# Two edits to a one-core attention and two-MLP kernel: other buffers for the last evacuations of the first MLP, and four of sixteen weight-conversion units issued in its last block

## The chip, the core and the metric

The kernel runs on one core of a Trainium2 chip. Five engines work side by side, each in its own program order: PE (TensorE matmuls; its weight loads are listed as PEld), DVE (VectorE), ACT (ScalarE), POOL (GpSimd) and SP (SyncE, which here only issues transfers). They wait for each other through semaphores. The metric is the device time of one execution in microseconds (us). Lower is better.

## The reference, cut to what matters

```python
# attention: 4 batches, 8 heads, 576 tokens, head size 64; block-causal mask in blocks of 64
scores = scale * np.matmul(q, k.transpose(0, 1, 3, 2))
scores = np.where(block_i >= block_j, scores, -1000000000.0)
attn = np.exp(scores - max); attn = attn / (sum(attn) + 1e-09)
x = np.matmul(attn, v)             # as a 2304 x 512 matrix
# first MLP: 512 -> 2048 -> 512
r = np.maximum(x @ w_in, 0.0)
x = (s * (r * r) + b) @ w_out
# second MLP: 512 -> 2048 -> 512, other weights
h = x @ w2_in
out = np.maximum(0.01 * h, h) @ w2_out
```

All arrays are float32. The kernel splits each matmul operand into a high part and a rest and adds three products, so that the result has float32 accuracy.

## The kernel before, in words

**Blocks.** The 2304 tokens are cut into five blocks by token position: four of 512 tokens (128 positions of each of four batches) and one of 256. `ORDER = (0, 1, 2, 4, 3)` gives the order in which they are worked on; here they are called by their place in that order, so block 3 is the one of 256 tokens and block 4, the last, again has 512. In each block the first MLP walks over 16 chunks `f` of the 2048 inner features. `m_in` (L864) computes `h` (twelve matmuls: four pieces of `x`, three products each), ACT and DVE turn it into `g = relu(h)^2`, `gh` (the high part) and `gl` (the rest), and `m_out` (L903) adds `gh` and `gl` times the output weights into four PSUM banks `y0` to `y3`. While block `k` runs its MLP, the attention of block `k + 1` is woven between its matmuls (`later_block`). The last block has no attention beside it.

**End of a block.** After the 16th chunk the four `y` banks are scaled and copied to SBUF tiles `yo` (`evac`, L477, on ACT or DVE, whichever the planner picks), and each `yo` tile is stored to the DRAM tensor `yT` (L936). The `yo` tiles come from the pool `st`, which has two buffers.

**Second weights.** The second MLP uses a Winograd form of Strassen's scheme (seven products in place of eight), so its weights are needed in combined blocks. Sixteen "units" (`units`, L392) prepare them while the first MLP runs. A unit takes a slot of the pool `stg` (two buffers of 16 KB per partition), loads 64-bit words with four transfers (L417), decodes them (DVE L424, L427, L433; ACT L430), makes four combined blocks (DVE L441), splits them (ACT L447, DVE L448) and stores them to `u_in` (L453) or `u_out` (L458). Units 0 to 3 and 8 to 11 make input weights (`u_in`), units 4 to 7 and 12 to 15 output weights (`u_out`) of the first and the second half of the features.

**Second MLP.** It runs six steps (three groups of 768 tokens, two feature halves each). Its tiles `G`, `gh2`, `gl2`, `Y` and `w2` are in pools that are opened after the pools of the first MLP are closed (`G.gate`, near the end), in the same SBUF space on the left side: from low to high addresses `stg`, `gh`, `gl`, `g`, `st`, `xh`, `xl` before, and `w2`, `gh2`, `gl2`, `Y`, `G` after. A tile that takes over the bytes of an older one waits until the older one's last reader is done, and a store is a reader until it has landed. `load_units` (L965) loads the combined weights (`wi`, `wo`), and `x_load` loads `yT` back as `xr`.

**Order.** No engine's order is written by hand. Every operation is a `Step` with a due time; `Graph.order` (L87) walks an event list with assumed durations and, for each engine that is free, issues the ready step with the earliest due time. For steps that open a buffer of a pool, a free buffer must be there. The instructions then stand in that order on their engines, and a wait at the head of an engine's queue holds up all behind it.

Of the kernel before, what the change touches and what calls it, by code (L numbers as in the profile page):

```python
# [8 lines left out]
F32 = mybir.dt.float32  # L9
# [182 lines left out]
NB = 5  # L192
# [4 lines left out]
def kernel(  # L197
# [19 lines left out]
    NF = w1_out.shape[0] // 128  # L217
# [6 lines left out]
    KEEP = 4  # L224
    NH = 384
    WS = 12
    BACK = 20.0

    def sb(name, bufs):
        return ctx.enter_context(tc.tile_pool(name=name, bufs=bufs))  # L230
# [33 lines left out]
    def buf(key, shape, dt=F32, tag=None):  # L264
        return Buf(key, lambda: pools[key][0].tile(shape, dt, tag=key, name=tag or key))

    def bank(key, name):
        return buf(key, [128, 512], F32, name)
# [16 lines left out]
    begin, ut, t = [], [], 30.0  # L285
# [6 lines left out]
    def at(k, f):  # L292
        return begin[k] + f * ut[k]
# [5 lines left out]
    w_t, w_ok = {}, {}  # L299
# [67 lines left out]
    def walk(blk):  # L367
        return range(NF) if blk % 2 == 0 else range(NF - 1, -1, -1)

    def weights_at(blk, pos, f):  # L370

        if not blk:
            return
        if pos < NF - KEEP:
            w_t[blk, f] = w_t[blk - 1, f]
            for i in range(2):
                w_ok[blk, f, i] = w_ok[blk - 1, f, i]
            return
        slot = f if f < KEEP else f - NF + 2 * KEEP
        w = w_t[blk, f] = buf("w", [128, 4, 512], F32R, "w")  # L380
        a = G.add(
            {"SP": 0.65}, lambda e: e.dma_start(out=w().bitcast(F32).rearrange("p a n -> p (a n)"), in_=kept[slot]),
            [kept_ok[f], done[blk, pos - NF + KEEP]], [w], [], at(blk, pos) - 30, nbytes=1048576)
        for i in range(2):
            w_ok[blk, f, i] = a
# [3 lines left out]
    OUT7 = ("S1", "S2", "S3", "S4", "A11", "A12", "A22")  # L389
    unit_ok = {}  # L390

    def units():  # L392

        seq = [(half, kind, i) for half in range(2) for kind in range(2) for i in range(4)]
        t0, t1 = begin[1] - 15, begin[NB] - 40
        stored = w_ok[0, NF - 1, 1]
        for n, (half, kind, i) in enumerate(seq):
            due = t0 + (n + 1) * (t1 - t0) / len(seq)
            slot = buf("stg", [128, 2, 2, 1024], F32, "unit")
            f1 = 8 * half + 2 * i  # L400
            at8 = (IN7, OUT7)[kind]
# [2 lines left out]
            blk = lambda x, slot=slot, names=names: slot()[:, 1, :, 128 * names.index(x):128 * names.index(x) + 128]  # L404
# [44 lines left out]
            st = []  # L449
# [27 lines left out]
    def evac(e, out, in_, by=1.0):  # L477
        if e is nc.scalar:
            e.activation(out=out, in_=in_, func=ACTF.Copy, scale=by)  # L479
        elif isinstance(by, float):  # L480
            e.tensor_copy(out=out, in_=in_)
        else:
            e.tensor_scalar(out=out, in0=in_, scalar1=by, scalar2=None, op0=ALU.mult)

    def both(n):
        return {"ACT": act(n), "DVE": dve(n)}
# [94 lines left out]
    for i in range(WARM + FILL):  # L581

        n = 128 if i < WARM else 256
# [46 lines left out]
    for p in range(NP):  # L630
        due = 10.0 + 4.0 * p
# [14 lines left out]
        o = bank("s", "o")  # L646
# [200 lines left out]
    def x_split(blk, c):  # L847

        k = ORDER[blk]
        T = TB[k]  # L850
        xf, ok = xf_t[k, c], xf_ok[k, c]
        x_open(blk, c)
        h, l = xh_t[blk, c], xl_t[blk, c]
        due = begin[blk] - 1
        hi = G.add({"ACT": act(T)}, lambda e: e.activation(out=h()[:, :T], in_=xf()[:, :T], func=ACTF.Copy), ok, [h], [xf], due)
        lo = G.add(
            {"DVE": dve(T)}, lambda e: e.tensor_tensor(out=l()[:, :T], in0=xf()[:, :T], in1=h()[:, :T].bitcast(F32), op=ALU.subtract),  # L857
            [hi], [l], [h, xf], due, port=True,
        )
        x_ok[blk, c] = [hi, lo]  # L860
# [40 lines left out]
    done = {}  # L901

    def m_out(blk, f, pos):  # L903
        k = ORDER[blk]
        T = TB[k]
        w = w_t[blk, f]
        W = T + 2 * (k == NB - 1)
        gh, gl, hi, lo = g_t[blk, f]
        due = at(blk, pos) + 1.5 * unit[k]
        for d in range(KD):  # L910
            if pos == 0:
                y_t[blk, d] = bank(f"y{d}", "y")
            y = y_t[blk, d]

            def fn(e, d=d, y=y):
                for n, (wi, x) in enumerate(((2, gh), (3, gh), (2, gl))):
                    e.matmul(  # L917
                        out=y()[:, :W], lhsT=w()[:, wi, d * 128:(d + 1) * 128], rhs=x()[:, :W],
                        start=(pos == 0 and n == 0), stop=(pos == NF - 1 and n == 2),
                    )  # L920

            a = G.add(
                {"PE": 3 * (T / 2400 + 0.013)}, fn, [hi, lo, w_ok[blk, f, 1], y_last.get((blk, d))],
                [y] * (pos == 0), [y, w, gh, gl], due + d * 0.01,
            )
            y_last[blk, d] = a
            if pos < NF - 1:
                continue
            o = buf("st", [128, 512], F32, "yo")
            ev = G.add(both(T), lambda e, o=o, y=y: evac(e, o()[:, :T], y()[:, :T], s_sb), [a, *sb_ok], [o], [y], due)  # L930
            if k == NB - 1:
                c_ok.append(G.add({"DVE": 0.2}, lambda e, y=y, d=d: e.tensor_scalar(
                    out=c_sb[:, d:d + 1], in0=y()[:, T:T + 1], scalar1=b_sb, scalar2=None, op0=ALU.mult), [a, *sb_ok], uses=[y], due=due))
            rows = slice(d * 128, (d + 1) * 128)
            y_st[k, d] = G.add(
                {"SP": 0.65}, lambda e, o=o, rows=rows: e.dma_start(out=yT[rows, T0[k]:T0[k] + T], in_=o()[:, :T]),  # L936
                [ev], uses=[o], due=due, nbytes=512 * T,
            )
        done[blk, pos] = a

    units()
    for blk in range(NB):
        if blk:
            for c in range(KD):
                x_split(blk, c)
        for pos, f in enumerate(walk(blk)):
            weights_at(blk, pos, f)
            m_in(blk, f, pos)
            m_out(blk, f, pos)
# [298 lines left out]
```

## Time and profile before

| | |
|---|---|
| median of 3 runs | 981.56 us (979.61 to 983.95) |
| profiled execution, its own time | 977.85 us |
| its span, first to last instruction | 975.9 us |
| PE busy | 942.3 us (97%) |
| PE weight loads busy | 828.6 us (85%) |
| DVE busy | 657.4 us (67%) |
| ACT busy | 576.3 us (59%) |
| mean granted TensorE clock | 0.995 of full speed |

Busy times are of one profiled execution on the hardware. A line number is that of the kernel before; `x3` after a row is the number of instructions merged into it, and in square brackets stands how long the engine had been idle and what ended that.

### The profile page before, as it was taken

Reading aid. Unit: us, or ns where it says so; the run is one execution under the profiler, and the core shown is the slowest. Engines: PE = TensorE matmul, PEld = TensorE weight load, DVE = VectorE, ACT = ScalarE, POOL = GpSimd, SP = SyncE. Lnnn points to the kernel's source line nnn. Section 1 sums busy time; section 2 is a strip of 40 time slices with the busy share of each in tenths; the row PEclk is TensorE's granted clock in tenths of the full one; section 3 lists DMA queues with packets and bytes.
Section 4 is the critical chain, followed back from the end, with each engine's and each line's share of the span. In section 5 each row is a group of like instructions: output and inputs, shape, how many; then the busy total and the mean of one; then the engine's idle time right before and its main releaser. Section 6 shows DMA issues by size and latency. Waiting matters only on the chain. (4 is left out here: it accounts for less than half of the span.)

```text
span 975.9 us, 16708 instructions
## 1 busy us (share of the span) xinstructions
PE 942.3 (97%) x5780; PEld 828.6 (85%) x5780; DVE 657.4 (67%) x1343; ACT 576.3 (59%) x1247; POOL 106.2 (11%) x231
## 2 busy tenths in 40 slices
PE   9899999999999999998999998899989999899998
PEld 8688887777778888786778887899979999799998
DVE  5888868668878687886866422456595565955657
ACT  4787757566677566876765321554564545645443
POOL 1122211111112131132220000000000000000000
PEclk9999999999999999999999999899999999999999
DMA  8994386976688967799745446774115751157402
GB/s 227 342 347 133 127 258 201 361 221 211 196 262 267 321 212 244 233 294 266 196 120 195 178 159 233 293 284 178 57 34 183 282 179 57 33 185 282 171 1 66
DMA packets 143828, 197.26 MB, mean 202 GB/s; under 512 B 23296, under 2 KB 118144, under 8 KB 137088
## 3 DMA queue, kind: packets, MB, share of 16 engines
q1 hardware_dynamic: 141296, 195.41, 61.1%
q10 hardware_dynamic: 2448, 0.79, 0.4%
q8 instruction: 46, 0.75, 0.3%
q14 instruction: 38, 0.31, 0.1%
HBM read 148.96 MB, written 47.19 MB: 201 GB/s over the span
## 5 line engine op out<-in xcount | busy, mean ns | idle before, releaser
L874 PE MATMUL h<-xh,w 128*128 128x512 f32 (+1 forms) x640 | 231.1, 390 | 5.1 <-DVE g L888 3.5
L917 PE MATMUL y<-gh,w 128*128 128x512 f32 (+1 forms) x640 | 186.0, 374 | 0.2 <-ACT gh L892 0.2
L874 PEld LDWEIGHTS h<-xh,w 128*128 128x128 f32 x640 | 118.4, 189 | 31.3 <-issue 5.2
L917 PEld LDWEIGHTS y<-gh,w 128*128 128x128 f32 x640 | 114.5, 188 | 22.2 <-issue 2.3
L1147 ACT ACTIVATE gh<-G 128x384 fp32r<-128x384 f32 x168 | 86.8, 524 | 59.1 <-PE A L1154 25.5
L1001 DVE TENSOR_TENSOR gl<-G,gh 128x384 fp32r<-128x384 f32 x168 | 92.5, 554 | 43.3 <-PE A L1154 18.7
L1088 PE MATMUL A<-xh,wi 128*128 128x384 f32 x384 | 112.9, 337 | 6.6 <-ACT G L1063 6.6
L874 PE MATMUL h<-xl,w 128*128 128x512 f32 (+1 forms) x320 | 118.5, 370 | 0.6 <-DVE xl L857 0.6
L917 PE MATMUL y<-gl,w 128*128 128x512 f32 (+1 forms) x320 | 118.5, 370 | 0.3 <-DVE l L763 0.3
L1154 PE MATMUL A<-gh,wo 128*128 128x384 f32 x384 | 98.4, 337 | 1.5 <-ACT gh L1147 1.5
L890 ACT ACTIVATE g<-h 128x512 f32<-128x512 f32 (+1 forms) x80 | 44.4, 554 | 85.5 <-PE h L874 78.9
L1088 PEld LDWEIGHTS A<-xh,wi 128*128 128x128 f32 x384 | 71.1, 189 | 7.0 <-ACT G L1063 6.9
L563 PE MATMUL t<-id_sb,p 128*128 128x128 f32 x400 | 66.6, 280 | 5.2 <-POOL p L765 1.9
L1154 PEld LDWEIGHTS A<-gh,wo 128*128 128x128 f32 x384 | 69.0, 188 | 2.8 <-ACT gh L1147 2.1
L917 PEld LDWEIGHTS y<-gl,w 128*128 128x128 f32 x320 | 60.2, 188 | 11.1 <-issue 0.4
L1103 ACT ACTIVATE G<-G 128x384 f32<-128x384 f32 x72 | 37.8, 525 | 52.1 <-DVE G L1068 52.1
L563 PEld LDWEIGHTS t<-id_sb,p 128*128 128x128 f32 x400 | 47.9, 142 | 22.0 <-issue 4.8
L874 PEld LDWEIGHTS h<-xl,w 128*128 128x128 f32 x320 | 60.6, 189 | 6.9 <-DVE xl L857 0.8
L1154 PE MATMUL A<-gl,wo 128*128 128x384 f32 x192 | 64.7, 337 | 0.4
L479 ACT ACTIVATE pt<-t 128x512 f32<-128x512 f32 (+2 forms) x80 | 42.4, 533 | 37.9 <-PE t L563 37.1
L1088 PE MATMUL A<-xl,wi 128*128 128x384 f32 x192 | 64.7, 337 | 0.0
L888 DVE TENSOR_TENSOR g<-g,h 128x512 f32<-128x512 f32 (+1 forms) x38 | 25.3, 665 | 54.8 <-ACT g L890 54.6
(125 smaller groups left out, 1894.3 us busy)
## 6 DMA issues: line engine op xcount, KB each, us to landing
wi<-u_in SPq DMA_DIRECT2D x32, 896.0 KB, 4.6
wo<-u_out SPq DMA_DIRECT2D x28, 1024.0 KB, 6.1
w<-kept SPq DMA_DIRECT2D x16, 1024.0 KB, 7.3
u_in<-unit SPq DMA_DIRECT2D x16, 896.0 KB, 5.7
u_out<-unit SPq DMA_DIRECT2D x32, 448.0 KB, 4.6
early<-in_moe_w_in_dram SPq DMA_DIRECT2D x16, 512.0 KB, 5.8
early<-in_moe_w_out_dram SPq DMA_DIRECT2D x16, 512.0 KB, 6.4
kept<-w SPq DMA_DIRECT2D x8, 1024.0 KB, 6.5
```

What stands on the lines that cost most here:

```text
L479: e.activation(out=out, in_=in_, func=ACTF.Copy, scale=by)
L563: e.transpose(tb()[:, x * 128:(x + 1) * 128], P()[:, pc:pc + 128], id_sb)
L874: e.matmul(out=h()[:, :T], lhsT=w()[:, wi, c * 128:(c + 1) * 128], rhs=x[blk, c]()[:, :T], start=(c == 0 and n == 0), stop=(c == KD - 1 an ...
L888: e.tensor_tensor(out=g()[:, :T], in0=g()[:, :T], in1=h()[:, :T], op=ALU.mult)
L890: a = G.add({"ACT": act(T)}, lambda e: e.activation(out=g()[:, :T], in_=h()[:, :T], func=ACTF.Relu), [prev], [g], [h], due)
L917: e.matmul(out=y()[:, :W], lhsT=w()[:, wi, d * 128:(d + 1) * 128], rhs=x()[:, :W], start=(pos == 0 and n == 0), stop=(pos == NF - 1 and n ...
L1001: e.tensor_tensor(out=out, in0=x, in1=y, op=ALU.subtract)
L1088: e.matmul(out=x()[:, :NH], lhsT=in_w[n, i, c]()[:, s, ai], rhs=y(), start=(first and c == 0 and m == 0), stop=(c == 1 and m == 2), skip_g ...
L1103: {"ACT": act(NH)}, lambda e, y=y: e.activation(out=y(), in_=y(), func=ACTF.Lrelu), [a], [], [y], d2 + 2)
L1147: hi = G.add({"ACT": act(NH)}, lambda e, gh=gh, x=x: e.activation(out=gh(), in_=x(), func=ACTF.Copy), [a], [gh], [x], due - 2)
L1154: e.matmul(out=z[d]()[:, :NH], lhsT=out_w[n, r]()[:, 2 * i + d, s], rhs=y(), start=(first and i == 0 and m == 0), stop=(i == 3 and m == 2) ...
```

## The change

There are two edits.

The four `yo` tiles of the last block come from the pool `xl` (four buffers) and no longer from `st` (two buffers). `xl` holds the rests of the block's input `x`, which `m_in` of the last chunk reads for the last time.

`units` is cut in two calls. Units 0 to 11 are added before the blocks, with due times spread between a little before block 1 and a little before block 3. Units 12 to 15 are added at block 4, with due times spread over block 4; their loads wait in addition for the step `done[NB - 2, 12]`, the last `m_out` matmul of the 13th chunk of block 3. The constant `BACK`, which nothing uses, goes.

```diff
-    BACK = 20.0
+    UNITS = 12
...
-    def units():
+    def units(which, stored):
 
         seq = [(half, kind, i) for half in range(2) for kind in range(2) for i in range(4)]
-        t0, t1 = begin[1] - 15, begin[NB] - 40
-        stored = w_ok[0, NF - 1, 1]
-        for n, (half, kind, i) in enumerate(seq):
-            due = t0 + (n + 1) * (t1 - t0) / len(seq)
+        first = (0, UNITS, len(seq))
+        spans = ((begin[1] - 15, begin[3] - 10), (begin[4] + 4, begin[5] - 6))
+        for n, (half, kind, i) in enumerate(seq[first[which]:first[which + 1]]):
+            due = spans[which][0] + (n + 1) * (spans[which][1] - spans[which][0]) / (first[which + 1] - first[which])
             slot = buf("stg", [128, 2, 2, 1024], F32, "unit")
...
-            o = buf("st", [128, 512], F32, "yo")
+            o = buf("st" if blk < NB - 1 else "xl", [128, 512], F32, "yo")
...
-    units()
+    units(0, w_ok[0, NF - 1, 1])
     for blk in range(NB):
+        if blk == NB - 1:
+            units(1, done[NB - 2, 12])
         if blk:
```

Since the planner sets the order, the change moves instructions on every engine from block 1 on. Three places follow. From the end of the first MLP on, PE's order is the same in both, row for row; the lines after the edit have moved by two numbers (L1063 is L1065, and so on).

ACT at the end of the last block, before (`g`, `gh`: last chunk; `yo`: evacuations; `G`: first tiles of the second MLP):

```order
L890 ACTIVATE g<-h 128x512
L892 ACTIVATE gh<-g 128x512
L479 ACTIVATE yo<-y,s_sb 128x512
L1063 ACTIVATE G<-A 128x384
L1063 ACTIVATE G<-C 128x384
L1103 ACT_TABLE_LOAD
L1103 ACTIVATE G<-G 128x384
```

and with the change:

```order
L890 ACTIVATE g<-h 128x512
L892 ACTIVATE gh<-g 128x512
L479 ACTIVATE yo<-y,s_sb 128x512 x2
L1065 ACTIVATE G<-A 128x384
L1065 ACTIVATE G<-C 128x384
L1105 ACT_TABLE_LOAD
L1105 ACTIVATE G<-G 128x384
```

ACT now does two of the four evacuations and DVE two, where it was one and three. Listed with its waits, the first `G<-A` waits for four transfers before, and for none with the change; in the program before, that `G` tile lies over both buffers of `st`. With the change the fifth to the tenth `G` tile lie over buffers of `xl`, and there a transfer is waited for.

SP at the end of block 3, before (`v`, `k`, `q`: attention loads; `unit`: loads of a unit; `u_out`: its stores; `yT`: stores of the block's result; `xr`: loads of the second MLP's first input):

```order
L708 DMA k<-in_k_dram 64x512 x2
L716 DMA v<-in_v_dram 128x4x128 x2
L458 DMA u_out<-unit 128x7x128 x4
L716 DMA v<-in_v_dram 128x4x128
L936 DMA yT<-yo 128x256 x2
L1023 DMA xr<-yT 128x384 x4
L936 DMA yT<-yo 128x256 x2
```

and with the change:

```order
L708 DMA k<-in_k_dram 64x512 x4
L716 DMA v<-in_v_dram 128x4x128 x2
L417 DMA unit<-in_moe_w_out_dram 128x2x256 x8
L716 DMA v<-in_v_dram 128x4x128
L936 DMA yT<-yo 128x256 x3
L1025 DMA xr<-yT 128x384
L936 DMA yT<-yo 128x256
```

The stores of the last unit are gone from here, and the eight loads of units 12 and 13 stand between the second-last and the last `v` load.

DVE from the end of block 3 into block 4, before (`xf`, `xl`: input of block 4; `c_sb`: a bias; `l`, `p`: softmax):

```order
L765 TENSOR_SCALAR p<-p,l 128x512
L857 TENSOR_TENSOR xl<-xf,xh 128x512 x3
L893 TENSOR_TENSOR gl<-g,gh 128x256
L481 COPY xf<-o 128x256
L483 TENSOR_SCALAR yo<-y,s_sb 128x256
L932 TENSOR_SCALAR c_sb<-y,b_sb 128x1
L483 TENSOR_SCALAR yo<-y,s_sb 128x256
L932 TENSOR_SCALAR c_sb<-y,b_sb 128x1 x3
L857 TENSOR_TENSOR xl<-xf,xh 128x512
L483 TENSOR_SCALAR yo<-y,s_sb 128x256 x2
L888 TENSOR_TENSOR g<-g,h 128x512
L893 TENSOR_TENSOR gl<-g,gh 128x512
```

and with the change:

```order
L427 SCALAR_TENSOR_TENSOR unit<-unit 128x1024
L441 TENSOR_TENSOR unit<-unit 128x2x128
L483 TENSOR_SCALAR yo<-y,s_sb 128x256
L857 TENSOR_TENSOR xl<-xf,xh 128x512
L448 TENSOR_TENSOR unit<-unit 128x2x896
L888 TENSOR_TENSOR g<-g,h 128x512
L433 SCALAR_TENSOR_TENSOR unit<-unit 128x2x512
L893 TENSOR_TENSOR gl<-g,gh 128x512
L441 TENSOR_TENSOR unit<-unit 128x2x128 x4
L893 TENSOR_TENSOR gl<-g,gh 128x512
L448 TENSOR_TENSOR unit<-unit 128x2x896
L893 TENSOR_TENSOR gl<-g,gh 128x512
```

Operations of units 12 and 13 now stand between the steps that feed the first chunks of block 4. Units 14 and 15 follow in the same way later in the block.

## Rows read from the trace of the kernel before

**Rows 1.** Busy time by stretch: length, engines' busy us (instructions), PE clock, DMA share, GB/s

```profile
405.00:515.00 110.00, 101.08 (x895) 85.00 (x895) 81.69 (x193) 74.11 (x174) 29.44 (x63) 0.98 0.75 218
515.00:605.00 90.00, 90.00 (x407) 75.22 (x407) 36.50 (x64) 30.51 (x56) 0.00 (x0) 1.00 0.55 189
605.00:616.00 11.00, 4.38 (x17) 4.06 (x17) 2.06 (x3) 3.58 (x6) 0.00 (x0) 0.69 1.00 379
616.00:976.00 360.00, 348.25 (x1983) 342.85 (x1981) 226.09 (x439) 192.25 (x399) 0.00 (x0) 1.00 0.41 148
```

**Rows 2.** Timeline, PE at the seam: start, us, engine, line, operation [idle before, releaser]

```profile
604.59 0.39 PE L917 MATMUL y<-gl,w 128*128 128x512 f32 x1
...
605.70 0.34 PE L1088 MATMUL A<-xh,wi 128*128 128x384 f32 x1
...
612.66 0.69 PE L1088 MATMUL A<-xh,wi 128*128 128x384 f32 x1 [6.62 <-ACT G L1063]
...
615.88 0.34 PE L1088 MATMUL C<-xl,wi 128*128 128x384 f32 x1
```

**Rows 3.** Timeline, ACT at the seam

```profile
603.66 0.69 ACT L479 ACTIVATE yo<-y,s_sb 128x512 f32<-128x512 f32 x1 [3.54 <-PE y L917]
612.11 0.49 ACT L1063 ACTIVATE G<-A 128x384 f32<-128x384 f32 x1 [7.77 <-DMA yT<-yo]
...
613.00 1.28 ACT L1103 ACT_TABLE_LOAD   x1
614.30 0.52 ACT L1103 ACTIVATE G<-G 128x384 f32<-128x384 f32 x1
```

**Rows 4.** Timeline of SP's last stores, and landing times of all stores of yo

```profile
606.67 1.08 SPq L936 DMA_DIRECT2D yT<-yo  x2
...
DMA to landing us min/median/max: 1.7/3.1/4.7
```

**Rows 5.** Timeline, four of PE's waits in block 3

```profile
410.12 0.39 PE L874 MATMUL h<-xl,w 128*128 128x256 f32 x1 [0.59 <-DVE xl L857]
...
452.76 0.33 PE L563 MATMUL t<-id_sb,p 128*128 128x128 f32 x1 [0.89 <-POOL p L765]
...
457.92 0.39 PE L874 MATMUL h<-xh,w 128*128 128x256 f32 x1 [1.90 <-DVE g L888]
...
506.94 0.39 PE L874 MATMUL h<-xh,w 128*128 128x256 f32 x1 [1.11 <-DVE g L888]
```

**Rows 6.** DVE's waits in block 3 (405 to 515): total us, times, longest

```profile
DVE unit L424 <- DMA unit<-in_moe_w_out_dram: 5.0, 2, 3.2
...
DVE unit L448 <- ACT unit L447: 2.0, 1, 2.0
```

**Rows 7.** Busy time by stretch of 5 us, columns as in rows 1

```profile
455.00:460.00 5.00, 3.10 (x21) 2.57 (x21) 3.85 (x10) 2.79 (x9) 2.61 (x5) 0.87 0.70 192
460.00:465.00 5.00, 5.00 (x49) 4.12 (x51) 2.57 (x7) 3.24 (x8) 0.00 (x0) 0.79 0.79 244
...
540.00:545.00 5.00, 5.00 (x24) 4.14 (x23) 3.77 (x7) 2.47 (x6) 0.00 (x0) 1.00 0.58 210
```

**Rows 8.** The units' instructions alone: length, DVE busy, ACT busy, clock, DMA share, GB/s

```profile
405.00:515.00 110.00, 25.43 (x30) 10.18 (x7) 0.98 0.75 218
...
sum 563.00, DVE 109.18 ACT 45.32; mean DVE 21.84 ACT 9.06
```

**Rows 9.** Timeline, one chunk of the last block on ACT and DVE

```profile
592.32 0.60 ACT L890 ACTIVATE g<-h 128x512 f32<-128x512 f32 x1 [3.46 <-PE h L874]
...
592.95 0.69 DVE L888 TENSOR_TENSOR g<-g,h 128x512 f32<-128x512 f32 x1 [3.36 <-ACT g L890]
...
593.67 0.63 ACT L892 ACTIVATE gh<-g 128x512 fp32r<-128x512 f32 x1 [0.75 <-DVE g L888]
...
594.33 0.69 DVE L893 TENSOR_TENSOR gl<-g,gh 128x512 fp32r<-128x512 f32 x1 [0.70 <-PE y L917]
```

**Rows 10.** Landing times of the units' loads (L417)

```profile
DMA to landing us min/median/max: 2.8/4.3/7.9
```

## The prediction

> **What bounds the kernel now.** I read the page's table of slices first, then busy time by stretch, then PE's waits in the stretches where it is not busy, and last the timelines of those places. In every stretch but two PE has work all the time. In the 90 us of block 4 it is busy 90.00 us, while DVE works 36.50 us and ACT 30.51 us [rows 1]. The two holes are block 3, with 101.08 us of 110 and a clock of 0.98, and the seam between the MLPs, with 4.38 us of 11 and a clock of 0.69 [rows 1]. Behind the seam PE has 348.25 us of 360, and that part keeps its order. So time is won only in those two holes, and lost only where PE begins to wait elsewhere.
>
> **First edit: the seam.** The last matmul before the hole starts at 605.70 and lasts 0.34 us; the next starts at 612.66, and the row gives 6.62 us of idle, ended by ACT's first G copy [rows 2]. That copy had waited 7.77 us for a yT store [rows 3]. The last two stores are issued together at 606.67 over 1.08 us, behind evacuations that needed the two st buffers back, and 4.7 us is the longest landing of such a store [rows 4]: 607.4 + 4.7 = 612.1, when the copy starts. After the hole PE runs at the low level: ten matmuls (A six, C four) take from 612.66 to 615.88 = 3.22 us; those after them start 0.17 us apart, so ten would take 1.75 us and 1.47 us is lost [rows 2]. Both together: 8.1 us.
>
> With the change the four evacuations need no store to land, and the G tiles that the first copies write lie over bytes that nobody holds; the fifth and later ones lie over xl. What is late next is ACT itself. The last y matmul ends at 604.59 + 0.39 = 604.98 [rows 2]; ACT's second evacuation takes 0.69 us and the G copy 0.49 us [rows 3], so PE can go on at about 606.2, 0.2 us after its last matmul of the row before. Later PE needs the copy behind the table load and the activation: 606.6 + 1.28 + 0.52 + 0.49 = 608.9, against about 608.3 when PE gets there, another 0.6 us. I leave 0.8 us, so the edit gives 7.3 us. Bounds: 8.1 us if none of this shows, 4.5 us if the fifth G tile must wait for a store with the longest landing (4.7 us) while big loads run beside it.
>
> At the table load a page of the Trainium skill speaks against the edit. In the row, the activation starts 0.02 us after the load ends (613.00 + 1.28 = 614.28, then 614.30) [rows 3]. The Trainium skill, "ScalarE: Activation LUTs", section "What ACT_TABLE_LOAD costs", counts about 1.38 us of drain to each such load besides its 1.28. By that the edit would give 5.9 us; the row shows no drain, and the sum goes by the row.
>
> **Second edit, what goes: block 3.** PE idles 110 - 101.08 = 8.9 us there [rows 1]. The first and the last wait that I show, 0.59 and 1.11 us [rows 5], belong to the block's input and to the last attention unit; 7.2 us are left. Of these, 0.89 us (the normalized p) and 1.90 us (g) [rows 5] come behind a DVE that stood at a unit's load: 5.0 us in two waits, and 2.0 us more for a unit's ACT step [rows 6]. Behind the 1.90 us the clock falls to 0.87 and 0.79 in two stretches of 5 us [rows 7], which is (0.13 + 0.21) x 5 = 1.7 us. So at most 7.2 + 1.7 = 8.9 us can go. In the same block units hold DVE for 25.43 and ACT for 10.18 us [rows 8], and with the change none of that is there until the block's last quarter. But the planner makes a new order, whose own late steps I can't see, and attention with its short chains stays. I take two thirds, 5.9 us, with bounds 0 and 8.9.
>
> **What comes: units 12 and 13.** On SP eight loads now wait for the 13th chunk of block 3. Queued behind them are the last v load, block 3's yT stores and the xr loads; the last v is needed only after the 16th chunk, so three chunks cover the eight issues and the landing. On DVE the first unit step waits for four of these loads. Behind it stand the last softmax of the block, then xl and g. The planner puts it there for loads that land at once; the rows say 4.3 us at the median and 7.9 at most [rows 10]. The nearest wait of this kind was 3.2 us [rows 6] and the PE waits behind such were 0.89 and 1.90 us [rows 5]. I take 1.5 us, bounds 0 and 3.2. Then come the first chunks of block 4. A chunk's chain from relu to gl takes 594.33 + 0.69 - 592.32 = 2.7 us [rows 9], and PE has 24 matmuls per chunk, 24 x 90.00 / 407 = 5.3 us [rows 1], so 2.6 us of cover. A unit is 109.18 / 16 = 6.8 us of DVE and 45.32 / 16 = 2.8 us of ACT [rows 8], in steps of up to 2 us, and in the new order one such step stands ahead of g and one ahead of gl. Two of them can eat the cover and a little more; I take 1 us for units 12 and 13 together, bounds 0 and 4.
>
> **Units 14 and 15** come when the block has settled. In 540 to 545 DVE had 3.77 us of work and PE still 5.00 [rows 7]; one step per half chunk fits under the cover. I put 0.3 us, bounds 0 and 2. Their loads and stores join the wi loads on SP in a block whose DMA share is 0.55 [rows 1]. POOL has no unit work. Units 0 to 11 were done by the end of block 2 before too; they only move closer together, which I put at 0, with 1.5 us either way for the new order of blocks 1 and 2, where PE has no hole to win.
>
> **Sum.** -7.3 - 5.9 + 1.5 + 1.0 + 0.3 = -10.4 us. Against the profiled execution's own 977.85 (span 975.9 and 1.95 around it) that is 967.4. That execution was 3.7 us under the median of the runs, 981.56, so for a median I expect 981.6 - 10.4 = 971.
>
> **Rivals.**
> 1. *The seam only.* The waits of block 3 return elsewhere: the new order packs attention and MLP as tightly as the old, and DVE is late for other reasons. For it: most of block 3's waits name g, p and pt, steps that stay. Against it: the 5.0 and 2.0 us of DVE standing at units [rows 6]. Time: 981.6 - 7.3 + 2.8 = 977.
> 2. *No gain at the seam.* The G copies meet the stores of the xl buffers at once, and the hole moves to the fifth G copy. Against it: each store now leaves as soon as its bank is copied, and ACT and DVE copy two banks each. Block 3 alone: 981.6 - 5.9 + 2.8 = 978.5.
> 3. *The table load holds ACT longer.* If ACT stands idle behind the load as long again as the load, 1.28 us, PE's second wait grows by it: 981.6 - 10.4 + 1.3 = 972.5. The drain that the Trainium skill counts ("ScalarE: Activation LUTs", section as above) is such a case; the row of the activation speaks against it [rows 3].
> 4. *Slower: the last block becomes DVE's.* Block 4 is the one stretch without any hole. Four units bring 4 x (6.8 + 2.8) = 38 us of DVE and ACT steps into chains that run one after another. It decides when the steps ahead of g and gl exceed 2.6 us in a chunk; if half of the 38 us comes on the path, 19 us, and block 3 gives its 5.9: 981.6 - 7.3 - 5.9 + 19 = 987. Against it: from 515 on DVE already carried such extra work (the splits of xr) with PE full.
>
> **Numbers.** The forecast 971 has 0.66 (its own range 966 to 975); rival 1 has 0.19, rival 2 0.05, rival 3 0.05, rival 4 0.05. Less than 0.5% (4.9 us) can't be told from no change, so faster means under 976.7. Forecast and rival 3 lie there nearly always (0.69), rival 1 half the time: 0.78 faster. Rivals 1 and 2 fill most of "same", 0.17; rival 4 gives slower, 0.05. Eight times in ten: the low end takes the full 8.9 us of block 3 and a cheap block 4 (981.6 - 8 - 8.9 + 1 = 965.7), less 2 us for the scatter of the runs, 963.5; the high end takes in rival 1 and a bit, 978.
>
> **What would show it.** At the seam, PE's wait on the G copy under 1 us, no wait of ACT on a yT store, and a clock of 1.00 there. In block 3, no DVE wait on a unit's load before its last quarter, PE busy over 106 us of 110, and no dip of the clock. At the start of block 4, one or two PE waits on g or xl, together about 2.5 us, with unit steps of DVE just ahead. I am wrong if a hole of several us stays at the seam (another tile's bytes), if block 3 idles as before without units, or if PE in block 4 waits in most chunks.

## The result, and the profile after

The changed kernel takes 967.23 us, median of its runs, against 982.75 us beside it: ratio 0.9844, 95% interval 0.9808 to 0.9880. Timed once more (e4 below) it is 965.94 against 983.34, ratio 0.9819, 0.9797 to 0.9842. The forecast was 971, its range 963.5 to 978. The profiled execution of after takes 969.23 us (span 967.2), so the two profiles are only 8.7 us apart in span, where the medians are 15.5 us apart. In the profiles 4.8 us are lost in block 0, which that of before leaves at 155.66 us and that of after at 160.43; from there on they differ by 13.5 us. The profile of before also flatters it: of its 47 executions timed beside the experiments the six with a mean granted clock of 0.994 or more take 979.3 us in the mean and the 14 with 0.990 or less 985.2 us, while the profiled one, at 0.995, takes 977.85 us and is faster than all of them.

Busy time by stretch of after, for [rows 1], with the same columns:

```profile
405.00:515.00 110.00, 109.24 (x957) 93.82 (x957) 74.96 (x205) 69.80 (x174) 28.11 (x64) 1.00 0.49 148
515.00:605.00 90.00, 88.66 (x405) 73.42 (x402) 50.87 (x76) 46.72 (x76) 0.00 (x0) 1.00 0.89 296
605.00:616.00 11.00, 10.79 (x61) 10.46 (x62) 5.70 (x11) 7.38 (x15) 0.00 (x0) 1.00 0.98 369
616.00:967.00 351.00, 339.60 (x1933) 334.38 (x1931) 220.94 (x429) 187.68 (x390) 0.00 (x0) 1.00 0.42 151
```

The two holes are closed: 0.8 us of idle in place of 8.9, 0.2 in place of 6.6, the clock at 1.00 in both. In the last block DVE and ACT have some 15 us more work each, and the DMA share is 0.89 in place of 0.55.

The seam, for [rows 2]: PE's timeline of after.

```profile
603.31 0.39 PE L917 MATMUL y<-gl,w 128*128 128x512 f32 x1
603.54 0.34 PE L1090 MATMUL A<-xh,wi 128*128 128x384 f32 x1
...
604.42 0.88 PE L1090 MATMUL A<-xh,wi 128*128 128x384 f32 x2
605.14 0.34 PE L1090 MATMUL A<-xl,wi 128*128 128x384 f32 x1
...
606.90 0.34 PE L1090 MATMUL C<-xh,wi 128*128 128x384 f32 x1
607.45 0.44 PE L1090 MATMUL A<-xh,wi 128*128 128x384 f32 x1 [0.21 <-ACT G L1065]
607.74 0.34 PE L1090 MATMUL A<-xl,wi 128*128 128x384 f32 x1
```

and ACT's, for [rows 3]:

```profile
603.74 0.69 ACT L479 ACTIVATE yo<-y,s_sb 128x512 f32<-128x512 f32 x1 [0.67 <-PE y L917]
604.32 0.48 ACT L1065 ACTIVATE G<-A 128x384 f32<-128x384 f32 x1
...
605.21 1.28 ACT L1105 ACT_TABLE_LOAD   x1
606.50 0.52 ACT L1105 ACTIVATE G<-G 128x384 f32<-128x384 f32 x1
```

The G copy follows the evacuation at once; it waits for no store. Two short waits of PE on G copies are left. Where it waits for nothing, these matmuls start 0.18 us apart (ten steps from 605.14 to 606.90); the two steps from 604.42 to 605.14 take 0.72 us and those from 606.90 to 607.74 take 0.84, in place of 0.35 each. So some 0.85 us are lost there in all, of which the view lists 0.21 as idle time.

The activation starts 0.01 us after the table load ends, so the drain that the Trainium skill counts ("ScalarE: Activation LUTs", section "What ACT_TABLE_LOAD costs") does not show here either.

Where the time went is best seen by block, from the first yT store of one block to that of the next. Blocks 1 to 4 of before (columns as in [rows 1]):

```profile
155.66:280.55 124.89, 124.81 (x753) 96.40 (x753) 95.54 (x218) 85.45 (x181) 21.95 (x39) 1.00 0.74 234
280.55:404.43 123.88, 122.59 (x862) 101.27 (x859) 94.14 (x204) 84.82 (x188) 23.66 (x56) 1.00 0.84 261
404.43:515.54 111.11, 102.19 (x901) 85.76 (x900) 82.78 (x196) 75.22 (x175) 29.44 (x63) 0.98 0.74 216
515.54:603.75 88.21, 88.21 (x397) 73.63 (x396) 35.98 (x63) 29.38 (x56) 0.00 (x0) 1.00 0.55 188
```

and of after:

```profile
160.43:286.01 125.58, 125.58 (x760) 97.47 (x760) 96.59 (x218) 86.72 (x187) 21.92 (x39) 1.00 0.76 238
286.01:414.68 128.67, 123.89 (x877) 99.93 (x874) 92.71 (x198) 81.24 (x178) 21.97 (x57) 1.00 0.76 238
414.68:512.84 98.16, 97.40 (x861) 84.10 (x858) 65.64 (x177) 62.94 (x158) 27.36 (x63) 1.00 0.52 159
512.84:602.48 89.64, 88.40 (x421) 73.54 (x420) 51.74 (x81) 45.77 (x75) 0.00 (x0) 1.00 0.87 291
```

Block 3 is 13.0 us shorter: 8.2 us are idle time of PE (111.11 - 102.19 = 8.9 before, 0.8 after), 4.8 us work that now stands elsewhere (901 matmuls, then 861; blocks 2 and 4 have more) or ran at a full clock. Block 2 pays 4.8 us, 3.5 of them idle; blocks 1 and 4 pay 0.7 and 1.4. Blocks 1 to 4 together gain 448.1 - 442.05 = 6.0 us, the seam and the second MLP 372.15 - 364.7 = 7.4.

### The profile page after: what moved, and what is told of

Read it like the earlier page. It is cut to its first block, busy times and chain, and to the rows that moved or that the text cites. A ratio compares the mean times of both kernels' runs of the same rounds, so it can differ in the third digit from the quotient of the medians.

```text
span 967.2 us, 16689 instructions
## 1 busy us (share of the span) xinstructions
PE 940.6 (97%) x5780; PEld 826.7 (85%) x5780; DVE 655.7 (68%) x1342; ACT 579.3 (60%) x1247; POOL 103.6 (11%) x232
## 5 line engine op out<-in xcount | busy, mean ns | idle before, releaser
L1149 ACT ACTIVATE gh<-G 128x384 fp32r<-128x384 f32 x168 | 86.8, 524 | 59.3 <-PE A L1156 25.4
L1156 PE MATMUL A<-gh,wo 128*128 128x384 f32 x384 | 98.4, 337 | 1.5 <-ACT gh L1149 1.5
L893 DVE TENSOR_TENSOR gl<-g,gh 128x512 fp32r<-128x512 f32 (+1 forms) x80 | 51.4, 643 | 16.5 <-ACT gh L892 14.1
```

The lines of the kernel that those rows point to most:

```text
L893: lo = G.add({"DVE": dve(T)}, lambda e: e.tensor_tensor(out=gl()[:, :T], in0=g()[:, :T], in1=gh()[:, :T].bitcast(F32), op=ALU.subtract), [ ...
L1149: hi = G.add({"ACT": act(NH)}, lambda e, gh=gh, x=x: e.activation(out=gh(), in_=x(), func=ACTF.Copy), [a], [gh], [x], due - 2)
L1156: e.matmul(out=z[d]()[:, :NH], lhsT=out_w[n, r]()[:, 2 * i + d, s], rhs=y(), start=(first and i == 0 and m == 0), stop=(i == 3 and m == 2) ...
```

## The experiments

Two questions: do the two edits add, and is it the unit work that made block 3's holes? The block bounds of all runs are found as above, and idle is block length less PE's busy time. Two profiles of one order differ by 0.5 us or more (block 3 of before and e1: 8.9 and 9.5; block 2 of after and e4: 4.8 and 4.1). Idle leaves out what a low clock costs: block 2 of e2 idles 1.8 us less than that of after, but at a clock of 0.97 it takes 128.9 us, no less than after's 128.7. Idle in us; "units" is DVE's time on unit steps in block 3:

| run | ratio to before (95%) | idle, blocks 1 / 2 / 3 / 4 | length of block 3 | units |
|---|---|---|---|---|
| before | 1 | 0.1 / 1.3 / 8.9 / 0.0 | 111.1 | 25.4 |
| after | 0.9844 (0.9808-0.9880) | 0.0 / 4.8 / 0.8 / 1.2 | 98.2 | 4.2 |
| e1 yo only | 0.9906 (0.9877-0.9935) | 0.1 / 1.1 / 9.5 / 0.0 | 111.8 | 25.4 |
| e2 units only | 0.9900 (0.9878-0.9922) | 0.0 / 3.0 / 0.7 / 1.2 | 98.1 | 4.2 |
| e3 all early | 0.9981 (0.9956-1.0006) | 1.7 / 8.1 / 5.8 / 0.0 | 109.1 | 2.0 |
| e4 after again | 0.9819 (0.9797-0.9842) | 0.0 / 4.1 / 0.7 / 1.2 | 98.1 | 4.2 |
| e5 before, empty units | 0.9967 (0.9948-0.9986) | 0.1 / 1.7 / 8.5 / 0.0 | 109.8 | 0 |
| e6 after, empty units | 0.9822 (0.9802-0.9841) | 0.0 / 4.3 / 0.6 / 0.5 | 97.7 | 0 |
| e7 old spacing | 0.9812 (0.9786-0.9837) | 0.1 / 1.3 / 2.6 / 1.2 | 99.6 | 4.2 |
| e8 eight late | 1.0189 (1.0156-1.0223) | 0.3 / 0.2 / 0.8 / 1.2 | 98.4 | 4.2 |
| e9 before, no transfers | 1.0203 (1.0168-1.0238) | 0.1 / 1.8 / 6.5 / 23.0 | 106.4 | 0 |
| e10 before, no stores | 1.0191 (1.0151-1.0232) | 0.1 / 1.1 / 6.9 / 23.0 | 108.4 | 25.4 |
| e11 ten, six | 0.9812 (0.9781-0.9842) | 0.1 / 1.2 / 3.4 / 0.0 | 102.3 | 22.0 |
| e12 eleven, five | 0.9881 (0.9861-0.9901) | 0.0 / 5.0 / 4.2 / 0.3 | 101.0 | 10.6 |

**e1 and e2: one edit at a time; e4: both.**

```diff
 e1, in before:
-            o = buf("st", [128, 512], F32, "yo")
+            o = buf("st" if blk < NB - 1 else "xl", [128, 512], F32, "yo")
 e2, in after: the same line the other way
```

> Only the first edit: the four last evacuations of the first MLP go into the xl buffers, all sixteen units stay where the kernel before has them. Apart from one evacuation that ACT does in DVE's place, every engine's instructions stand in the same order as before. Theory (the two edits add): the seam gives 7.4 us, what the two profiles show between the last yT stores and the end, and nothing else moves: 7 to 8 us under the kernel before, ratio 0.992. Rival (the edits need each other, because unit stores and loads also lie in the queues at the seam): under 5 us. Rival (the seam gives more in the median than in the two profiles, and block 3 less): over 10 us.

> Only the second edit: twelve units early, four from the end of block 3, the last evacuations stay in the st buffers. Apart from one evacuation, the order on every engine is that of the changed kernel. Theory (the edits add): the hole of 6.6 us at the seam with its low clock is back, and what remains is the 15.5 us of both less 7.4: 8 us under the kernel before, ratio 0.992; block 3 is as short as in the changed kernel (98 us between first yT stores) and block 2 as long (129 us). Rival (seam larger): 3 to 5 us under the kernel before.

> The changed kernel once more, beside the others on one chip. Theory: 15 us under the kernel before, ratio 0.984 (first result 0.9844, 0.9808 to 0.988). Its block 0 in a second profile tells whether the 4.8 us by which it came later out of block 0 than the kernel before, with the same order there, belong to the execution: if so block 0 ends within 2 us of 155.7; if it belongs to the program, near 160.4 again.

Medians: 973.38 (e1), 973.62 (e2) and 965.94 us (e4), against 983.34. The product of the two ratios is 0.981, e4's is 0.982: the edits add. From the last block's first yT store to the end e1 takes 364.7 us as after does, e2 373.2 (before 372.2). In time by the medians each edit gives about 10 us, more than the 7 to 8 us expected of each and than the 7.4 and 6 us of the profiles; e1's interval (6.4 to 12.1 us) holds its 7.4. That the profile of before flatters it may be why; no run shows it. The stretch of the seam in e1 and in e2, one row each:

```profile
600.00:616.00 16.00, 15.68 (x80) 13.98 (x79) 6.39 (x11) 7.96 (x15) 0.00 (x0) 1.00 0.80 274
```

```profile
600.00:616.00 16.00, 9.68 (x36) 8.92 (x35) 3.78 (x6) 4.79 (x8) 0.00 (x0) 0.68 0.95 373
```

e2 has the hole and the low clock back, e1 neither. On block 0, e4 gave no clear answer: it ends at 158.72, between the two first profiles.

**e3: no unit in blocks 3 and 4.**

```diff
-    UNITS = 12
+    UNITS = 16
-            units(1, done[NB - 2, 12])
+            pass
```

> Both edits, but no unit is held back: all sixteen are spread over blocks 1 and 2, and neither block 3 nor block 4 has any. Theory (block 3 gains because no unit's load or step stands ahead of its chains on DVE and ACT): block 3 stays at 96 to 99 us between first yT stores, the start of block 4 wins its 1.4 us, and blocks 1 and 2 pay for a third more unit work, 0 to 5 us: 11 to 17 us under the kernel before. Rival (the gain is the new order of blocks 2 and 3, which the due times of the twelve units happened to bring): block 3 comes back to 105 us or more, and the whole lies 7 to 10 us under the kernel before, hardly more than the seam alone.

981.69 against 983.34 us: nearly all of the gain is gone, less than either side had expected, though the seam is as good as in after (365.0 us to the end). Blocks 1 and 2, with a third more unit work, take 260.4 us in place of 248.8, where 0 to 5 us more were allowed for, and block 2 idles 8.1 us; but block 3 too, with one unit step left in it, idles 5.8 us:

```profile
420.45:529.56 109.11, 103.34 (x919) 87.19 (x918) 68.27 (x185) 65.69 (x165) 27.22 (x63) 1.00 0.51 151
```

That speaks against my theory, but e3 also has another order of steps. So the next runs keep the order.

**e5 and e6: the order kept, the unit steps emptied.** A step that the planner has placed issues no instruction:

```diff
-                e.tensor_scalar(out=word(0), in0=word(0), scalar1=29, ...
+                empty or e.tensor_scalar(out=word(0), in0=word(0), scalar1=29, ...
 and so for every DVE and ACT step of units 12 to 15
-                 in_=part()[:, c].rearrange("p (r n) -> p r n", r=7)
+                 in_=id_sb[:].unsqueeze(1).to_broadcast([128, 7, 128]) if empty else ...
```

> The kernel before, its order untouched, but units 12 to 15 do none of their steps on DVE and ACT; their loads stay and their stores send a constant tile of the same size, so part of the second weights is not converted. In the profile of before block 3 idles PE for 8.9 us, of 111.1. Theory U (the unit steps on DVE and ACT make those holes, as the prediction had it): idle in block 3 falls to 3 us or less, the block to 102 to 105 us, the whole by 6 to 9 us. Rival O (the holes belong to the order in which attention and MLP steps stand on PE, DVE and POOL, and the change won by making another order; the run with all units early speaks for it, where block 3 had no units and still idled 5.8 us): idle stays at 6 us or more and the whole falls by 3 us at most.

> The changed kernel, its order untouched, but units 12 to 15 do none of their steps on DVE and ACT (loads stay, stores send a constant tile). The price of these units at the start of block 4 is what comes off. In the changed kernel block 4 idles 1.24 us and the whole block takes 89.65. Theory: both waits of PE there (0.5 us on the block's input, 0.8 us on g) go, block 4 takes 88.2 to 88.6, and the whole is 1 to 1.5 us under the changed kernel, 964 to 965; block 3 gives nothing, since only its last 15 us held a unit. Rival (transfers of the units, not their steps, disturb block 4: DMA share 0.88 to 0.92 there): block 4 stays at 89.6.

e5: 979.67 against 983.65 us. DVE's busy time in block 3 falls from 82.8 to 60.4 us, and PE's idle time only from 8.9 to 8.5:

```profile
407.94:517.77 109.83, 101.35 (x901) 85.73 (x900) 60.39 (x166) 65.87 (x168) 27.35 (x63) 0.98 0.75 219
```

So taking away DVE's and ACT's unit steps, at whose loads DVE stood for 5.0 us [rows 6], gives back almost none of it, no more than two profiles differ by: theory U fell. (The whole falls by 4.0 us, interval 1.4 to 5.1, where rival O had 3 at most; block 3 is only 1.3 us shorter.) Just ahead of the 1.90 us hole of [rows 5] stand three shorter waits in before, 0.60, 0.89 [rows 5] and 0.34 us:

```profile
446.44 0.66 PE L563 MATMUL t<-id_sb,p 128*128 128x128 f32 x4 [0.60 <-ACT pt L479]
...
453.43 0.55 PE L563 MATMUL t<-id_sb,p 128*128 128x128 f32 x3 [0.34 <-POOL p L765]
```

All three are gone in e5, 1.83 us together, and the hole is 1.84 us longer. The name at its end leads elsewhere; PE, ACT and SP of e5:

```profile
460.79 0.39 PE L874 MATMUL h<-xh,w 128*128 128x256 f32 x1 [3.74 <-DVE g L888]
```

```profile
459.38 0.63 ACT L678 ACTIVATE kh<-k 128x512 fp32r<-128x512 f32 x1 [2.12 <-DMA k<-in_k_dram]
459.92 0.36 ACT L890 ACTIVATE g<-h 128x256 f32<-128x256 f32 x1
```

```profile
452.83 1.19 SPq L458 DMA_DIRECT2D u_out<-id_sb  x2
454.12 2.49 SPq L708 DMA_DIRECT2D k<-in_k_dram  x2
```

ACT stood at a k load with g queued behind it, and SP had issued that load behind units' stores. e6: 965.75 us, against 965.94 for after; block 4 is 0.36 us shorter than in e4 (89.65 to 89.29), where 1.0 to 1.4 was expected. The wait on g goes, the 0.5 us on the block's input stays.

**e9 and e10: the transfers too.** e9 drops the loads of units 12 to 15 as well and sends their stores together after block 3; e10 keeps loads and steps and only moves the stores (a constant tile, as above):

```diff
+    late = lambda e, *a: send(e, *a) if flushed else held.append(a)
+    flush = lambda e: (flushed.append(len(held)), [send(e, *a) for a in held])
 the last yT store of block 3 calls flush; in e9 the loads are "empty or e.dma_start(...)"
```

> The kernel before in its order, with units 12 to 15 as empty as in e5 and their loads gone as well; their stores go out together behind the last yT store of block 3, so that SP and the DMA queues have no unit work in block 3. In e5, with the steps gone, block 3 still idled 8.48 us; its longest hole, 3.7 us, ends with ACT's step on k, which had stood 2.1 us for a k load that SP issued behind four stores and two loads of units. Theory D (the units' transfers in SP's queue make block 3's holes: loads of q and k come late, ACT and DVE stand at them, g is late): idle in block 3 falls to 3 us or less and the block to 103 to 105 us, against 109.8 in e5; block 4 may pay some us for the stores put together. Rival O (the order of the steps itself): idle stays at 6 us or more, the block at 108 us or more.

> The kernel before in its order; units 12 to 15 are loaded and do all their steps, but their sixteen stores go out together, from a constant tile, behind the last yT store of block 3. It halves theory D: if the stores (917 KB a pair, 1.8 MB a unit) hold up SP, the loads of k come sooner, DVE's steps stay, and block 3 idles 4 to 6 us in place of 8.9; if it is the loads of units, which wait for a free buffer at the head of SP's queue, nothing is won: 8 us or more.

The totals (1004.11 and 1003.60 us, before 984.73) are spoilt by the stores put together, see the end; block 3 is what they were made for. e9, blocks 3 and 4:

```profile
406.29:512.64 106.35, 99.89 (x901) 84.77 (x900) 60.58 (x166) 65.84 (x168) 28.01 (x63) 1.00 0.43 127
512.64:626.42 113.78, 90.76 (x397) 75.13 (x396) 36.01 (x63) 29.50 (x56) 0.00 (x0) 0.90 0.66 211
```

and block 3 of e10:

```profile
406.76:515.19 108.43, 101.55 (x901) 85.71 (x900) 82.52 (x196) 74.64 (x175) 29.49 (x63) 0.98 0.52 154
```

Idle 6.46 us in e9, 6.88 in e10 (between its two expected ranges). The transfers cost 8.5 - 6.5 = 2.0 us, the stores alone as much (8.9 - 6.9); 6.5 us stay with no unit work, load or store in the block. They belong to the order: rival O, to which e9 gave 6 us or more (its length of 108 was set too high, since the clock is at 1.00 in e9). Block 3 of e6 is the counterpart, with the same steps empty, the transfers still there, but the order of after: 0.6 us of idle.

```profile
413.14:510.88 97.74, 97.11 (x861) 84.12 (x858) 61.63 (x173) 61.80 (x157) 25.80 (x63) 1.00 0.54 160
```

In e10 DVE does all its unit steps and never waits for a unit's load in block 3 (5.0 us in before); the three shorter waits are gone, as in e5, and the hole is that of before:

```profile
458.09 0.38 PE L874 MATMUL h<-xh,w 128*128 128x256 f32 x1 [1.89 <-DVE g L888]
```

The same hole on PE and ACT of e9:

```profile
457.14 0.39 PE L874 MATMUL h<-xh,w 128*128 128x256 f32 x1 [1.73 <-DVE g L888]
```

```profile
453.89 0.68 ACT L756 ACTIVATE p<-s,nm 128x512 f32<-128x512 f32 x1
...
454.55 0.69 ACT L756 ACTIVATE p<-s,nm 128x512 f32<-128x512 f32 x1
...
455.21 0.42 ACT L892 ACTIVATE gh<-g 128x256 fp32r<-128x256 f32 x1
455.52 0.63 ACT L678 ACTIVATE kh<-k 128x512 fp32r<-128x512 f32 x1
456.25 0.38 ACT L890 ACTIVATE g<-h 128x256 f32<-128x256 f32 x1
```

ACT is busy without a break from 453.89 on, and the softmax, gh and kh stand ahead of the g that PE waits for: 1.73 us without units, 1.90 with them.

**e7, e8, e11, e12: other due times.**

```diff
 e7 :  spans = ((begin[1] - 15, begin[1] - 15 + 0.75 * (begin[NB] - 25 - begin[1])), (begin[4] + 4, begin[5] - 6))
 e8 :  UNITS = 8
 e11:  UNITS = 10, units(1, done[NB - 2, 4]), second span from begin[4] - 60
 e12:  UNITS = 11, units(1, done[NB - 2, 8]), second span from begin[4] - 30
```

> The changed kernel with the first twelve units due at the intervals of the kernel before (they are not drawn together), so that blocks 1 and 2 are loaded as before and block 3 holds hardly any unit; the last four are still held back. Theory U: block 2 is back at 124 us with about 1.3 us of idle in place of 128.1 to 128.9, block 3 idles about as little as in the changed kernel; against the changed kernel 2 to 4 us are won: 962 to 964, the best so far. Rival O (block 3 depends on the order, not on the units): block 3 idles 5 us or more again and the whole is 968 to 975.

> The changed kernel with eight units held back in place of four. Theory: block 2 loses its extra idle (about 3 us), but block 4 becomes DMA's: four units raise its DMA share from 0.55 to 0.88, eight would ask for 1.2, so that block 4, or the stores behind it, takes 0.2 x 90 = 18 us more; the whole is about 980, and DVE waits for unit loads. Rival (the transfers fit, since the share counts waiting as work): block 4 stays at 90 to 93 us and the whole is 962 to 966.

> The changed kernel with ten units in blocks 1 and 2 and six from the fifth chunk of block 3 on, spread to the end of block 4. Theory D: two units among block 3's loads of q and k bring back a part of its holes, about 2 of the 8.2 us that went, and block 2 wins 2 to 3 us of its 4.1 us of idle; against the changed kernel no difference, within 3 us either way. Rival O (a step order with fewer units in block 3 is what counts, and each order has its own holes): anything from 955 to 975.

> The changed kernel with eleven units in blocks 1 and 2 and five from the ninth chunk of block 3 on, spread to the end of block 4. In e9 block 3 idled 6.5 us without any unit work or transfer in the order of before, and in e11 only 3.4 us with 22 us of unit work on DVE. Theory O (each set of due times makes another order, with holes of its own, and unit work on the chip hardly matters): the idle of blocks 1 to 4 together lies anywhere between 4 and 11 us and does not follow the unit work of a block; the whole 961 to 972. Theory U (unit work makes the holes): block 3 has some 14 us of it on DVE and idles between the 0.7 of the changed kernel and the 3.4 of e11, block 2 less than the 4.1 of the changed kernel, so that the whole is 961 to 966.

e7: 966.12 us, block 2 back at 124.9 as expected, but block 3 idles 2.6 us; the time lies in neither side's range. e11: 965.47 us. Neither can be told from after (965.94). In e11 theory D's numbers came true (block 3 idles 2.7 us more than in e4, block 2 2.8 us less), which is also near the 2.4 us that e5 and e9 give for unit work and its transfers. e11's block 3 shows the other half; its row, and that of the units' instructions in it (DVE, ACT):

```profile
408.31:510.65 102.34, 98.94 (x864) 84.55 (x862) 78.88 (x192) 72.53 (x171) 27.36 (x63) 1.00 0.71 218
```

```profile
408.31:510.65 102.34, 22.00 (x26) 8.73 (x7) 1.00 0.71 218
```

Nearly as much unit work as in before, and as high a DMA share (0.71, before 0.74), but 3.4 us of idle in place of 8.9. e12: 970.23 us against 982.39; with half of that unit work it idles more in block 3 (4.2) and 5.0 us in block 2, where unit work is a third less than in after. Theory U had 961 to 966, theory O 961 to 972, a range so wide that little could have spoken against it. e8: 1002.42 us, slower than its 980, and not where expected. Block 4 takes 89.8 us; only some four of the eight units get done there, and the steps of the rest stand on ACT ahead of the first G copy. PE's and ACT's timelines of e8:

```profile
632.92 0.69 PE L1090 MATMUL A<-xh,wi 128*128 128x384 f32 x1 [34.63 <-ACT G L1065]
```

```profile
617.07 1.10 ACT L430 ACTIVATE unit<-unit 128x1024 f32<-128x1024 f32 x1 [12.07 <-DMA u_out<-unit]
...
632.40 0.47 ACT L1065 ACTIVATE G<-A 128x384 f32<-128x384 f32 x1
```

The price that I had put on the DMA queues in block 4 came as a wait of 34.6 us at the seam: units' loads and stores ran at their pace, and the copies queued behind the units.

## Why the prediction was right, and where it was not

**The seam: right in mechanism and size.** Forecast 7.3 us, measured 7.4 (372.15 to 364.7), in e1 too. I left 0.2 + 0.6 = 0.8 us for waits on ACT's copies, and by the starts of the matmuls two waits cost some 0.85. Behind the seam PE does not have "work all the time": it idles 11.75 us in before and 11.40 in after, which is nearly the same.

**Block 3: the right sign, the wrong reason.** I read DVE's 5.0 and 2.0 us at units as the cause of PE's waits and took 5.9 us of 8.9. In block 3 alone 8.2 us of idle went. But in the order of before the unit steps account for 0.4 us of the idle and the transfers for 2.0 (e5, e9); 6.5 us lie in how attention and MLP steps stand on in-order engines, and they went because the planner, with other due times, wrote another order (6.5 us in e9, 0.6 in e6). What failed is the step by which the waits of 0.89 us (p) and 1.90 us (g) came behind a DVE that stood at a unit's load: the first is gone in e5, e9 and e10, the second in none of them, though DVE stands at no unit's load in any. Rival 1 held the true objection ("DVE is late for other reasons"); its conclusion, that the waits return, holds for e3 and in part for e12, not for this order.

**Blocks 1 and 2: outside their bounds.** I put 0, with 1.5 us either way. Block 2 idles 3.5 us more in after, 2.8 in e4. PE and DVE of after at its start:

```profile
291.60 0.50 PE L874 MATMUL h<-xl,w 128*128 128x512 f32 x1 [0.98 <-DVE xl L857]
293.50 0.40 PE L786 MATMUL s<-kh,qs 128*128 128x288 f32 x1 [1.17 <-ACT p L797]
```

```profile
288.92 2.02 DVE L448 TENSOR_TENSOR unit<-unit 128x1792 f32<-128x1792 f32 x1
290.86 0.69 DVE L857 TENSOR_TENSOR xl<-xf,xh 128x512 fp32r<-128x512 f32 x1
```

The 2.02 us unit step stands ahead of the split that PE waits for. It was not emptied by itself; that it makes this 0.98 us is read from the rows, not shown. Part of block 3's gain is given back here.

**Units 12 to 15: dearer in the forecast than on the chip.** Forecast 2.5 us for the first two and 0.3 for the last two; block 4 is 1.4 us longer, with 1.24 us of idle, all in two waits (0.48 us for the block's input, 0.76 for g behind another 2.03 us unit step) before 522. From 525 to 600 PE is busy throughout, so units 14 and 15 cost nothing there. The emptied steps give back 0.4 us in block 4 and as much in block 3 (e6). Of the two waits the one for the block's input stays with the steps empty, so only the one for g is theirs. Rival 4's slow last block did not come.

**The sum.** Forecast -10.4: seam -7.3, blocks 1 to 4 -3.1. Profiles: -7.4 and -6.0 (e4: -7.5 and -6.6). That blocks 1 to 4 came within 3 us of the forecast is luck: block 3 is 13.0 us shorter where I had 4.4 (5.9 less 1.5 for the loads of units 12 and 13), by another mechanism, and blocks 1, 2 and 4 are 6.9 us longer where I had 1.3 in block 4 and nothing in the others. By medians 15.5 and 17.4 us were won, 2 to 3 us more than the profiles show behind block 0. Part of that is likely that the profile of before flatters it, as said above; block 3 takes 0.7 us longer in e1. Its block 0, too, is the earliest of five profiles with its due times (155.7, 158.4, 158.8, 156.9, 158.2 us). What stays open: the nine profiles with other due times leave block 0 at 158.7 to 160.4, some 2 us later in the mean, though in after PE's order there is that of before; and which feature of an order decides its holes.

## What to carry to other kernels

The name at the end of a wait is the last one to arrive and need not be the cause: empty the suspected steps in an unchanged order before you price their removal. Where a planner writes the order, any change of due times rewrites all blocks behind it; price it by PE's idle time per block, before and after, and expect several us either way. Buffers that a phase's first tiles lie over are worth looking up one by one: that gain came as forecast, 7.4 us for 7.3.

## What the runs showed of the hardware that was not expected

Sixteen stores of 459 KB put together held SP for 23.67 us, 1.48 us an issue, where the units' own stores in before take 0.55 us each at the median (and 0.59 us in e5, from the same constant tile); the next loads waited behind them. SP's timeline of e9, the busy time in that stretch (columns as in [rows 1]), and two rows of its waits from 515 on:

```profile
516.43 23.67 SPq L296 DMA_DIRECT2D u_out<-id_sb  x16
540.15 3.97 SPq L1023 DMA_DIRECT2D xr<-yT  x4
```

```profile
516.43:540.10 23.67, 7.68 (x34) 6.01 (x33) 3.09 (x5) 4.03 (x8) 0.00 (x0) 0.74 1.01 290
```

```profile
ACT xr L1028 <- DMA xr<-yT: 25.2, 1, 25.2
...
PE y L917 <- ACT gh L892: 23.0, 1, 23.0
```

One 25 us wait of ACT, in the block that had no hole at all, became 23 us of idle PE. The DMA engines are full while the burst lasts (share 1.01, 290 GB/s), and 16 x 459 KB in 23.67 us are, as an estimate, 310 GB/s: SP issued the stores about as fast as their bytes moved. The block's mean share, 0.66, hides that.
